# A convolution and gated two-layer product: the first product's rest term as a pair of 64-row matmuls

## The chip, the core and the metric

The kernel runs on one core of one Trainium2 chip. A core has five engines that run side by side and meet only at semaphores: TensorE (PE in the profile, with its weight loads listed apart as PEld), VectorE (DVE), ScalarE (ACT), GpSimd (POOL), and SyncE (SP), which here only issues DMAs. PE multiplies a stationary block of weights (up to 128 rows by 128 columns) with moving columns and adds into PSUM. The metric is the device time of one execution in microseconds (us), lower is better. Before the change it is 2808.53 us, the median of three runs from 2807.76 to 2809.02.

## What is computed

```python
w = softmax(weight)                      # 8 heads, 7 taps each
x = causal_convolution(x, w)             # 8 x 4096 tokens, 192 channels, 24 per head
x = x.reshape(32768, 192)
h = x @ w_in                             # 192 x 2048
P = a[0] + a[1] * h + a[2] * h**2 + a[3] * h**3
Q = 1.0 + abs(b[0]) * abs(h) + abs(b[1]) * h**2
out = (P / (Q + 1e-6)) @ w_out           # 2048 x 192
```

## The kernel before

The tokens go in 64 chunks of 512. For each chunk the convolution is done on PE as band matrices (`conv_part`, L259): nine blocks of up to 58 tokens by six groups of 32 channels. Each matmul fills 32 columns of the array only, at `tile_position=(0, 32 * j)`. Half 0 has four groups, side by side on four column tiles, and gives 128 channels; half 1 has two groups on two column tiles and gives the last 64. In the trace each of these float32 matmuls stands as two instructions, and so does each of the second product's.

PE takes the first product in float32r, a shorter form of float32. So both of its factors are kept as two parts, a leading one and the rest: `wh_t` and `wl_t` for w_in, and for the convolved chunk ACT writes the leading part (`conv_evac_act`, L267, tiles xh0 and xh1) and DVE the rest (`conv_evac_dve`, L273 and L277). For the first 128 channels the parts are `xh0` (called A) and `xl` (L). For the last 64 channels one tile, `xh1` (B), holds the leading part in rows 0 to 63 and the rest in rows 64 to 127. The host lays out w_in's last 64 rows twice, so `wh_t[:, i, 1]` and `wl_t[:, i, 1]` hold the same 64 rows in both halves, and one pass over 128 rows multiplies both parts of B by one part of the weights.

The 2048 columns of w_in are taken in eight units of 256, two halves of 128 each. `gemm1(k, j)` (L289) makes half j of unit k: five full passes of 128 rows by 512 columns into one half of the PSUM tile hp, of which there are two. After that ACT, POOL and DVE work out P / (Q + 1e-6) for the unit in twelve or so steps of 128 x 1024 elements (L328 to L379), and `gemm2` (L306) multiplies the result with w_out, 64 float32 matmuls of 192 columns a chunk, spread between the units of the first product.

The order on PE, ACT, DVE and POOL is written out by hand as a list of steps: START (the first two chunks, with the weights' conversion from float64 in steps `wi..` and `wo..`), PLAN (one round, a chunk long, repeated), END. `g10a.0 ... g10b.0` is the first product's two halves of unit 0, `c1a.0` a third of the convolution's half 1, `xh1.0` and `xl1.0` its two evacuations by ACT and DVE. The order on SP is not in these lists: it is what the framework's scheduler makes of it. SP carries the loads of x (`load_x`, L158 and L159, into two buffers xs in turn, each needed again a round after it is filled or later) and the stores of the result (L314). In a round, `xl1.0` stands four steps before `g10a.0`, the first step that reads B:

```python
... c1a.0 c1b.0 L4.1 c1c.0 p6.1 m3.1 g17a.1 A6.1 g17b.1
e3.1 u6.1 xh1.0 B6.1 g24d.1 g3.1 p7.1 g25a.1 Q6.1 g25b.1 v6.1 Y4.1 g25c.1 hs7.1 xl1.0 g25d.1 m4.1
g10a.0 B7.1 u7.1 A7.1 g10b.0 e4.1 L5.1 g26a.1 ...
```

Of the kernel before, what the change touches and what calls it, by code (L numbers as in the profile page):

```python
# [10 lines left out]
F32 = mybir.dt.float32  # L11
F32R = mybir.dt.float32r
# [4 lines left out]
ALU = mybir.AluOpType  # L17
# [7 lines left out]
P = 128  # L25
CH = 512
# [11 lines left out]
F64_MIN = float(np.uint32(0x38000000).view(np.float32))  # L38


# The order in which the engines take the steps of one chunk of tokens: step, unit or half,
# piece; after the point, how many chunks later than the first step of its chunk it is taken.
PLAN = """
c0a.0 L7.2 m6.2 u1.1 g12a.1 O1.2 A1.1 e6.2 g12b.1 B1.1 Q0.1 g6.2 g20a.1 hs2.1 c0b.0 v1.1 g20b.1 Y7.2
c0c.0 p2.1 L0.1 m7.2 g13a.1 B2.1 u2.1 g13b.1 e7.2 A2.1 g20c.1 g7.2 A3.1 g20d.1 Q1.1 g21a.1 v2.1 Y0.1
# [6 lines left out]
g11a.0 m5.1 p0.0 B0.0 g11b.0 e5.1 u0.0 L6.1 g27a.1 g5.1 hs1.0 g27b.1 g27c.1 p1.0 v0.0 Y6.1 g27d.1  # L52
"""

# How a unit's cubic begins. H: on VectorE, from PSUM; U: on GpSimd; V: on ScalarE, then GpSimd.
MODES = "UUUHVUUV"

# The first two rounds, with the preparation of the weights (wi: w_in, wo: w_out; step, piece);
# after the point the chunk.
START = """  # L60
wia0.0 c0a.0 wim0.0 wis0.0 c1a.0 wid0.0 wia1.0 c1b.0 wio0.0 wim1.0 wir0.0 c1c.0 wis1.0 c0b.0 c0c.0
xh1.0 wid1.0 wia2.0 wih0.0 xl1.0 wio1.0 xh0.0 wir1.0 wim2.0 wid2.0 wia3.0 wil0.0 wia4.0 xl0.0 wis2.0
# [13 lines left out]
L6.0 e5.0 u0.1 wor7.0 hs1.1 g5.0 p1.1 Y6.0 v0.1 wor4.0  # L76
"""

# What remains after the last full round; after the point the chunks from the end.
END = """  # L80
u1.2 L7.3 m6.3 B1.2 O1.3 c0a.1 g12a.2 A1.2 g12b.2 Q0.2 e6.3 hs2.2 c0b.1 g6.3 Y7.3 g20a.2 v1.2 A2.2
B2.2 c0c.1 g20b.2 m7.3 g20c.2 p2.2 g20d.2 g21a.2 e7.3 g13a.2 g13b.2 g21b.2 g7.3 g21c.2 u2.2 xh0.1
# [26 lines left out]
def kernel(  # L109
# [12 lines left out]
    nc = tc.nc  # L122
# [3 lines left out]
    xpool = ctx.enter_context(tc.tile_pool(name="xpool", bufs=2))  # L126
# [9 lines left out]

    nc.scalar.preload_act_table_set("natural_log_exp_and_others")

# [1 line left out]
    wb_t = const.tile([P, NG, BW], F32, name="wb_t")  # L140
    mb_t = const.tile([P, NG, BW], F32, name="mb_t")
    wr_t = const.tile([P, NG, KT], F32, name="wr_t")
# [15 lines left out]
        nc.sync.dma_start(out=t[0:BLK, 0:3 * XF // 4], in_=xa[c])  # L158
        nc.sync.dma_start(out=t[BLK:, 3 * XF // 4:], in_=xb[c])  # L159

# [1 line left out]
    mx = const.tile([P, NG], F32, name="mx")  # L162
    sm = const.tile([P, NG], F32, name="sm")
    nc.vector.tensor_reduce(out=mx, in_=wr_t, axis=AX.X, op=ALU.max)
# [7 lines left out]
    nc.vector.tensor_tensor(out=wb_t, in0=wb_t, in1=mb_t, op=ALU.mult)  # L172
    nc.vector.tensor_tensor(out=wb_t, in0=wb_t, in1=sm[:, :, None].broadcast_to([P, NG, BW]), op=ALU.mult)

# [1 line left out]
    cf = const.tile([P, 6], F32, name="cf")  # L176
    nc.vector.tensor_scalar(cf[:, 0:4], ab_t[:, 0:4], -1.0, None, ALU.mult)
    nc.scalar.activation(out=cf[:, 4:6], in_=ab_t[:, 4:6], func=AF.Abs)
# [15 lines left out]
        scales.append(reg)  # L194
    r_be0, r_sq1, r_a3 = scales

# [1 line left out]
    # In integers: the upper word's digits, rebiased, then the lower word's, rounded, added.  # L198
    wh_t = const.tile([P, UPC, 2, 2, P], F32R, name="wh_t")
    wl_t = const.tile([P, UPC, 2, 2, P], F32R, name="wl_t")  # L200
    wo_t = const.tile([P, FT, D], F32, name="wo_t")
# [16 lines left out]
    def prep(which, i, step):  # L218
        w = pieces[which, i]
        if step == "a":  # L220
            ad = apool.tile([P, 2, W // 2], I32, name="ad")
            w["a"], w["d"] = ad[:, 0, 0:w["n"]], ad[:, 1, 0:w["n"]]
            nc.scalar.activation(out=w["a"].bitcast(F32), in_=w["hi"].bitcast(F32), func=AF.Abs)
        elif step == "d":
            nc.scalar.activation(out=w["d"], in_=w["lo"], func=AF.Identity, scale=2.0 ** -29)
        elif step == "m":
            nc.vector.tensor_scalar(w["a"].bitcast(F32), w["a"].bitcast(F32), F64_MIN, None, ALU.max)  # L227
        elif step == "s":
            if which == "i":
                w["t"] = apool.tile([P, W // 2], F32, name="tr")  # L230
            else:
                w["t"] = wo_t[:, 2 * i:2 * i + 2].rearrange("p f m -> p (f m)")
            nc.vector.tensor_scalar(w["t"].bitcast(U32), w["a"].bitcast(U32), 3, 0x3FFFFFF8,  # L233
                                    ALU.logical_shift_left, ALU.bitwise_and)
        elif step == "o":
            t = w["t"].bitcast(U32)
            nc.vector.scalar_tensor_tensor(out=t, in0=w["hi"], scalar=0xC0000000, in1=t,  # L237
                                           op0=ALU.bitwise_and, op1=ALU.bitwise_or)
        elif step == "r":
            t = w["t"].bitcast(I32)  # L240
            nc.gpsimd.tensor_tensor(out=t, in0=t, in1=w["d"], op=ALU.add)
        elif step == "h":
            nc.scalar.copy(out=wh_t[:, i].rearrange("p a b c -> p (a b c)"), in_=w["t"])
        elif step == "l":
            nc.vector.tensor_tensor(out=wl_t[:, i].rearrange("p a b c -> p (a b c)"), in0=w["t"],  # L245
                                    in1=wh_t[:, i].rearrange("p a b c -> p (a b c)").bitcast(F32), op=ALU.subtract)

# [1 line left out]
    def stat(c, blk, g):  # L249
        t = xs_buf[c % 2].rearrange("p (m b g) -> p m b g", m=32, b=NBLK)  # L250
        return t[:, :, blk, g]
# [10 lines left out]
    X = {}  # L262

    def conv_evac_act(c, half, cps):
        xh = xpool.tile([P, CH], F32R, name=f"xh{half}")
        n = 32 * len(GROUPS[half])
        nc.scalar.copy(out=xh[0:n], in_=cps[0:n])  # L267
        X[c, "AB"[half]] = xh

    def conv_evac_dve(c, half, cps):  # L270
        if half == 0:
            xl = xpool.tile([P, CH], F32R, name="xl")
            nc.vector.tensor_tensor(out=xl, in0=cps, in1=X[c, "A"].bitcast(F32), op=ALU.subtract)  # L273
            X[c, "L"] = xl
        else:
            xh = X[c, "B"]
            nc.vector.tensor_tensor(out=xh[64:P], in0=cps[0:64], in1=xh[0:64].bitcast(F32), op=ALU.subtract)  # L277

# [1 line left out]
    H = {}  # L280

    def gemm1(k, j):
        c, i = divmod(k, UPC)
        xhA, xlA, xB = X[c, "A"], X[c, "L"], X[c, "B"]
        if j == 0:
            H[k] = ps_h.tile([P, 2, CH], F32, name="hp")
        terms = ((wh_t, 0, xhA), (wh_t, 0, xlA), (wh_t, 1, xB), (wl_t, 0, xhA), (wl_t, 1, xB))
        for n, (w, part, x) in enumerate(terms):
            nc.tensor.matmul(H[k][:, j, :], lhsT=w[:, i, part, j, :], rhs=x, start=(n == 0), stop=(n == len(terms) - 1))  # L289

# [1 line left out]
    G = {}  # L292
    O = {}

# [18 lines left out]
        nc.scalar.copy(out=ob, in_=O.pop((c, pair))[:, :, 0:D])  # L313
        nc.sync.dma_start(out=out_v[c, pair], in_=ob)  # L314

# [1 line left out]
    st = {}  # L317

    def flat(k):
# [59 lines left out]
        nc.vector.scalar_tensor_tensor(out=g, in0=st[k]["y"], scalar=2.0, in1=g, op0=ALU.subtract, op1=ALU.mult)  # L379
        del st[k], H[k]  # L380

# [1 line left out]
    unit_steps = {"hs": step_hs, "p": step_p, "u": step_u, "v": step_v, "A": step_A, "B": step_B, "Q": step_Q,  # L383
                  "L": step_L, "Y": step_Y, "m": step_m, "e": step_e, "g": step_g}
    CP = {}
# [9 lines left out]
    def take(kind, n, piece, c):  # L395
        if kind in ("g2", "O"):
            if c > NCH or c < 0:
                return
            if kind == "g2":
                if c > 0:  # L400
                    gemm2(c - 1, n, piece)
            elif c > 0:
                out_evac(c - 1, n)
        elif 0 <= c < NCH:
            if kind == "g1":
                gemm1(c * UPC + n, piece)
            elif kind == "c":
                conv_step(c, n, piece)
            elif kind == "xh":
                conv_evac_act(c, n, CP[c, n])  # L410
            elif kind == "xl":
                conv_evac_dve(c, n, CP.pop((c, n)))
            else:
                unit_steps[kind](c * UPC + n)

# [1 line left out]
    def steps(text):  # L417
        return [(kind, int(n), "abcd".find(piece) if piece else 0, int(c))
                for kind, n, piece, c in re.findall(r"(g1|g2|w[io][a-z]|[A-Za-z]+)(\d)([a-d]?)\.(\d+)", text)]

    order = steps(START)
# [3 lines left out]
    with tc.manual_schedule(engines={E.PE, E.Activation, E.DVE, E.Pool}):  # L425
        load_x(0)
        for i in range(UPC):
            load_w("i", i)
        load_x(1)
        for i in range(UPC):  # L430
            load_w("o", i)
        for kind, n, piece, c in order:
            if kind[0] == "w":
                prep(kind[1], n, kind[2])
            else:
                take(kind, n, piece, c)
# [52 lines left out]
```

## Time and profile before

| what | us |
|---|---|
| runs, median of three | 2808.53 |
| the profiled execution: span from its first to its last instruction (no other time of it is given) | 2807.8 |
| second product, busy (L306, 8128 instructions) | 1420.8 |
| first product, leading weights by A and B, busy (L289, 2048 passes) | 872.9 |
| first product, rest weights by A and B, busy (2048 passes) | 637.7 |
| first product, leading weights by the rest of A, busy (1024 passes) | 405.5 |
| convolution, busy (L259, 6876 instructions) | 195.3 |

The busy times of PE's groups overlap, since one matmul starts before the end of the one ahead of it; what one costs is read from how far apart the starts lie. A row of the timeline has the start and the duration in us, the engine, the line, the operation, the tiles (written <- read), and how many instructions in a row it covers; in square brackets stand the idle time of the engine before it and what ended that. A row of a window has its length and then, for each engine, the busy time and the number of instructions. A row of the waits has the total in us, how many, and the longest.

### The profile page before, as it was taken

What the parts mean: (1) busy time and instruction counts of PE and PEld (TensorE: products, weight loads), DVE (VectorE), ACT (ScalarE), POOL (GpSimd) and SP (SyncE); (2) the same over time, 40 slices, a digit from 0 to 9 for tenths busy, and PEclk for the clock granted to TensorE, in tenths of its full rate; (3) what the DMA queues carried; (4) which work ended last, traced back from release to release, by engine and by line L of the source; (5) the groups of instructions that cost most, each with busy time, mean ns of one, the idle gap of its engine ahead of it and who ended that gap; (6) DMA issues with size and microseconds to landing.
All of it is one profiled execution on the core that took longest, in us unless ns stands there. A gap on an engine that the chain in (4) does not pass through costs nothing.

```text
span 2807.8 us, 50193 instructions
## 1 busy us (share of the span) xinstructions
PE 2748.3 (98%) x20224; PEld 2458.2 (88%) x20224; DVE 2683.3 (96%) x2309; ACT 2688.4 (96%) x2990; POOL 2684.4 (96%) x1304
## 2 busy tenths in 40 slices
PE   4799999999999999999999999999999999999999
PEld 3688988988889889889889888888898898898888
DVE  8999999999999999999999999999999999999998
ACT  6899999999999999999999999999999999999997
POOL 6899999999999999999999999999999999999996
PEclk8899999999999999999999999999999999999999
DMA  4000000000000000000000000000000000000000
GB/s 136 10 16 25 22 16 25 22 16 25 21 17 22 19 22 22 19 22 22 16 25 22 16 25 22 16 22 19 22 22 19 22 22 16 25 22 16 25 9 15
DMA packets 49193, 64.43 MB, mean 23 GB/s; under 512 B 4672, under 2 KB 43840, under 8 KB 48960
## 3 DMA queue, kind: packets, MB, share of 16 engines
q1 hardware_dynamic: 48960, 61.22, 7.9%
q8 instruction: 159, 2.61, 0.4%
q14 instruction: 74, 0.61, 0.1%
HBM read 36.03 MB, written 25.17 MB: 22 GB/s over the span
## 4 chain that ended last, share of the span: by engine, by line
PE 96%; DVE 2%; issue 1%; ACT 0%; DMA 0%; SPq 0%; ACTq 0%; DVEq 0%
PE op L306 48%; PE hp L289 42%; PE cps L259 6%; DVE ad L227 0%; PE cps L306 0%; DVE t L351 0%; DVE wl_t L245 0%; DMA g<-in_w_in 0%; DVE g L370 0%; DVE y L375 0%; DVE tr L233 0%; DVE tr L237 0%; DVE wo_t L233 0%; DVE g L379 0%; DVE wo_t L237 0%
## 5 line engine op out<-in xcount | busy, mean ns | idle before, releaser
L306 PE MATMUL op<-wo_t,g 128*128 128x192 f32 x8128 | 1420.8, 326 | 0.0
L306 PEld LDWEIGHTS op<-wo_t,g 128*128 128x128 f32 x8128 | 1344.6, 189 | 43.9
L360 POOL TENSOR_TENSOR A<-A,B 128x1024 f32<-128x1024 f32 x512 | 1219.2, 2388 | 28.4 <-ACT B L357 26.1
L347 POOL TENSOR_TENSOR t<-t,hs 128x1024 f32<-128x1024 f32 x448 | 1077.9, 2406 | 48.6 <-ACT hs L334 16.3
L289 PE MATMUL hp<-xh,wh_t 128*128 128x512 f32 x2048 | 872.9, 426 | 45.9 <-DVE t L351 41.4
L370 DVE SCALAR_TENSOR_TENSOR g<-t,cf,y 128x1024 f32<-128x1024 f32 x512 | 654.4, 1278 | 57.0 <-ACT y L366 46.6
L351 DVE SCALAR_TENSOR_TENSOR t<-t,cf,hp 128x1024 f32<-128x1024 f32 x512 | 652.5, 1274 | 32.7 <-POOL t L347 29.9
L379 DVE SCALAR_TENSOR_TENSOR g<-y,g 128x1024 f32<-128x1024 f32 x512 | 626.9, 1224 | 17.5
L289 PE MATMUL hp<-xh,wl_t 128*128 128x512 f32 x2048 | 637.7, 393 | 0.0
L375 DVE SCALAR_TENSOR_TENSOR y<-A,y 128x1024 f32<-128x1024 f32 x512 | 625.5, 1222 | 0.0
L363 ACT ACTIVATE B<-A 128x1024 f32<-128x1024 f32 x512 | 547.0, 1069 | 0.2 <-POOL A L360 0.2
L366 ACT ACTIVATE y<-B 128x1024 f32<-128x1024 f32 x512 | 528.8, 1033 | 15.6 <-DVE g L379 14.6
L354 ACT ACTIVATE A<-hp 128x1024 f32<-128x1024 f32 x512 | 528.0, 1031 | 15.8 <-PE hp L289 15.7
L357 ACT ACTIVATE B<-hp 128x1024 f32<-128x1024 f32 x512 | 528.7, 1033 | 0.0
L289 PEld LDWEIGHTS hp<-xh,wh_t 128*128 128x128 f32 x2048 | 388.8, 190 | 124.4 <-DVE t L351 32.6
L334 ACT COPY hs<-hp 128x1024 f32<-128x1024 f32 x448 | 457.2, 1020 | 35.4 <-PE hp L289 34.1
L289 PEld LDWEIGHTS hp<-xh,wl_t 128*128 128x128 f32 x2048 | 388.2, 190 | 87.5
L289 PE MATMUL hp<-xl,wh_t 128*128 128x512 f32 x1024 | 405.5, 396 | 2.4 <-DVE xl L273 2.4
L340 POOL TENSOR_SCALAR t<-hs,cf 128x1024 f32<-128x1024 f32 x320 | 389.6, 1217 | 10.8 <-ACT hs L334 3.9
L328 ACT ACTIVATE t<-hp,cf 128x1024 f32<-128x1024 f32 x192 | 214.7, 1118 | 25.3 <-PE hp L289 22.8
L259 PEld LDWEIGHTS cps<-wb_t,xs 128*32 128x32 f32 x6876 | 162.5, 149 | 65.8 <-issue 64.3
L289 PEld LDWEIGHTS hp<-xl,wh_t 128*128 128x128 f32 x1024 | 195.4, 191 | 23.7 <-DVE xl L273 2.9
(49 smaller groups left out, 632.6 us busy)
## 6 DMA issues: line engine op xcount, KB each, us to landing
out<-ob SPq DMA_DIRECT2D x128, 192.0 KB, 2.0
xs<-in_xa SPq DMA_DIRECT2D x64, 324.0 KB, 3.9
xs<-in_xb SPq DMA_DIRECT2D x64, 108.0 KB, 3.7
g<-in_w_in SPq DMA_DIRECT2D x8, 512.0 KB, 9.4
g<-in_w_out SPq DMA_DIRECT2D x8, 384.0 KB, 9.3
wb_t<-in_wband SPq DMA_DIRECT2D x1, 174.0 KB, 2.4
mb_t<-in_mband SPq DMA_DIRECT2D x1, 174.0 KB, 2.4
wr_t<-in_wrep SPq DMA_DIRECT2D x1, 21.0 KB, 1.9
```

Of the source, the lines that this page charges most:

```text
L289: nc.tensor.matmul(H[k][:, j, :], lhsT=w[:, i, part, j, :], rhs=x, start=(n == 0), stop=(n == len(terms) - 1))
L306: nc.tensor.matmul(op[:, t, 0:D], lhsT=g[:, f % 2, tok:tok + P], rhs=wo_t[:, f, :], start=(f == 0 and t == 0), stop=(f == FT - 1 and t == 1))
L347: nc.gpsimd.tensor_tensor(out=t, in0=t, in1=st[k]["hs"], op=ALU.mult)
L351: nc.vector.scalar_tensor_tensor(out=t, in0=t, scalar=a1, in1=flat(k), op0=ALU.add, op1=ALU.mult)
L354: nc.scalar.activation(out=tile_of(k, "A", work), in_=flat(k), func=AF.Abs, scale=r_be0)
L357: nc.scalar.activation(out=tile_of(k, "B", work), in_=flat(k), func=AF.Square, scale=r_sq1)
L360: nc.gpsimd.tensor_tensor(out=st[k]["A"], in0=st[k]["A"], in1=st[k]["B"], op=ALU.add)
L363: nc.scalar.activation(out=st[k]["B"], in_=st[k]["A"], func=AF.Ln, bias=C_Q)
L366: nc.scalar.activation(out=tile_of(k, "y", ps_y), in_=st[k]["B"], func=AF.Exp, scale=-1.0)
L370: nc.vector.scalar_tensor_tensor(out=G[k].rearrange("p a b -> p (a b)"), in0=st[k]["t"], scalar=a0, in1=st[k]["y"], op0=ALU.add, op1=ALU.mult)
L375: nc.vector.scalar_tensor_tensor(out=y, in0=st[k]["A"], scalar=C_Q, in1=y, op0=ALU.add, op1=ALU.mult)
L379: nc.vector.scalar_tensor_tensor(out=g, in0=st[k]["y"], scalar=2.0, in1=g, op0=ALU.subtract, op1=ALU.mult)
```

## The change

The line of `wl_t` for the last 64 channels gets a new upper half: after a unit's `wl_t` has been made, a DMA copies rows 0 to 63 of `wh_t[:, i, 1]` over it. B gets a new lower half: the leading part is copied by a DMA to rows 64 to 127. One full pass of `wl_t[:, i, 1]` with B now gives leading weights by leading x (upper half) plus rest weights by leading x (lower half), for which there were two passes. The rest of the last 64 channels goes to a tile of its own, `xm`: DVE writes rows 0 to 63, a DMA copies them to rows 64 to 127. A unit's last term, leading weights by xm, is a pair of 64-row matmuls after the second half's passes: rows 0 to 63 of the array for half 0, rows 64 to 127 for half 1, each of 512 columns into its own half of hp. The product of the rest weights with xm, which the pass before took along, is left out. So a unit has eight full passes and a pair instead of ten full passes. The lists START, PLAN and END stay.

```diff
         elif step == "l":
             nc.vector.tensor_tensor(out=wl_t[:, i].rearrange("p a b c -> p (a b c)"), in0=w["t"],
                                     in1=wh_t[:, i].rearrange("p a b c -> p (a b c)").bitcast(F32), op=ALU.subtract)
+            nc.sync.dma_start(out=wl_t[0:64, i, 1].bitcast(F32), in_=wh_t[0:64, i, 1].bitcast(F32))
...
         nc.scalar.copy(out=xh[0:n], in_=cps[0:n])
+        if half == 1:
+            nc.sync.dma_start(out=xh[64:P].bitcast(F32), in_=xh[0:64].bitcast(F32))
         X[c, "AB"[half]] = xh
...
-            xh = X[c, "B"]
-            nc.vector.tensor_tensor(out=xh[64:P], in0=cps[0:64], in1=xh[0:64].bitcast(F32), op=ALU.subtract)
+            xm = xpool.tile([P, CH], F32R, name="xm")
+            nc.vector.tensor_tensor(out=xm[0:64], in0=cps[0:64], in1=X[c, "B"][0:64].bitcast(F32), op=ALU.subtract)
+            nc.sync.dma_start(out=xm[64:P].bitcast(F32), in_=xm[0:64].bitcast(F32))
+            X[c, "M"] = xm
...
-        terms = ((wh_t, 0, xhA), (wh_t, 0, xlA), (wh_t, 1, xB), (wl_t, 0, xhA), (wl_t, 1, xB))
+        terms = ((wh_t, 0, xhA), (wh_t, 0, xlA), (wl_t, 0, xhA), (wl_t, 1, xB))
         for n, (w, part, x) in enumerate(terms):
-            nc.tensor.matmul(H[k][:, j, :], lhsT=w[:, i, part, j, :], rhs=x, start=(n == 0), stop=(n == len(terms) - 1))
+            nc.tensor.matmul(H[k][:, j, :], lhsT=w[:, i, part, j, :], rhs=x, start=(n == 0), stop=False)
+        if j == 1:
+            xlB = X[c, "M"]
+            for half in range(2):
+                rows = slice(64 * half, 64 * half + 64)
+                nc.tensor.matmul(H[k][:, half, :], lhsT=wh_t[rows, i, 1, half, :], rhs=xlB[rows], start=False, stop=True,
+                                 tile_position=(64 * half, 0))
```

On PE, this is the place in a round where a new chunk's unit 0 begins, before the change. The rows are PE's matmuls in program order, with the line, the tiles and the shape; xh_1572 is xh0 (A) of the new chunk and xh_1689 its xh1 (B); the number behind a tile only tells buffers apart, and 128x512 is the output's shape. First stand the last two passes of unit 7 of the chunk before.

```order
L289 MATMUL hp<-xh_1205,wl_t 128x512
L289 MATMUL hp<-xh_1322,wl_t 128x512
L306 MATMUL op<-wo_t,g 128x192 x10
L289 MATMUL hp<-xh_1572,wh_t 128x512
L289 MATMUL hp<-xl,wh_t 128x512
L289 MATMUL hp<-xh_1689,wh_t 128x512
L289 MATMUL hp<-xh_1572,wl_t 128x512
L289 MATMUL hp<-xh_1689,wl_t 128x512
```

The same place of the changed kernel; A of the new chunk is xh_1592 here and B xh_1709. What a row waits for is shown where it waits: DMAHW6 and DMAHW0 are the semaphores of DMAs, here those of the copies into B and into xm.

```order
L294 MATMUL hp<-xh_1339,wl_t 128x512
L299 MATMUL hp<-xm,wh_t 128x512 x2
L317 MATMUL op<-wo_t,g 128x192 x10
L294 MATMUL hp<-xh_1592,wh_t 128x512 [waits DVE_49,PE_49]
L294 MATMUL hp<-xl,wh_t 128x512
L294 MATMUL hp<-xh_1592,wl_t 128x512
L294 MATMUL hp<-xh_1709,wl_t 128x512 [waits DMAHW6_49,Activation_49]
L294 MATMUL hp<-xh_1592,wh_t 128x512
L294 MATMUL hp<-xl,wh_t 128x512
L294 MATMUL hp<-xh_1592,wl_t 128x512
L299 MATMUL hp<-xm,wh_t 128x512 [waits DVE_49]
L299 MATMUL hp<-xm,wh_t 128x512 [waits DMAHW0_49]
```

The pass of leading weights by B is gone from each half; the pair stands behind the second half's passes and ahead of the second product's matmuls, and the second one of it waits for the DMA into xm. The other engines keep their rows in their order.

On SP, these are the DMAs of one round before the change, in the order in which SP issues them: loads of x, then two stores.

```order
L158 DMA xs_97<-in_xa 64x1296
L159 DMA xs_97<-in_xb 64x432
L314 DMA out<-ob 128x2x192 x2
```

And of the changed kernel, with the copies into B (L270) and into xm (L281):

```order
L158 DMA xs_97<-in_xa 64x1296
L270 DMA xh_969<-xh_969 64x512
L159 DMA xs_97<-in_xb 64x432
L281 DMA xm<-xm 64x512
L325 DMA out<-ob 128x2x192 x2
```

The copy into B stands between the two loads of x, so the second load waits behind it; the copy into xm stands after both, ahead of the stores.

## The prediction

> **What bounds the kernel now.** I read the page's busy shares first, then one round of the loop (one chunk of 512 tokens) in the view of busy time by window, then the chain that ended last.
>
> ```profile
> span 2807.8 us, 50193 instructions
> PE 2748.3 (98%) x20224; PEld 2458.2 (88%) x20224; DVE 2683.3 (96%) x2309; ACT 2688.4 (96%) x2990; POOL 2684.4 (96%) x1304
> core 0: us, PE busy (x) PEld busy (x) DVE busy (x) ACT busy (x) POOL busy (x), PEclk, DMA share, GB/s
> 1480.00:1522.67 42.67, 42.67 (x318) 38.25 (x316) 41.05 (x36) 41.62 (x47) 41.52 (x21) 1.00 0.08 21
> 57.00:100.00 43.00, 19.12 (x73) 13.46 (x71) 42.80 (x41) 29.02 (x38) 34.55 (x20) 0.65 0.00 0
> PE 96%; DVE 2%; issue 1%; ACT 0%; DMA 0%; SPq 0%; ACTq 0%; DVEq 0%
> 114.73 3.90 PE op L306 x24
> 2675.40 3.90 PE op L306 x24
> ```
>
> Four engines stand at 96 to 98% of the span, so the shares alone don't say which one sets the time. The round does: PE is busy 42.67 of 42.67 us at granted clock 1.00, while ACT, POOL and DVE have 1.05, 1.15 and 1.62 us free. The chain agrees (96% PE), and its two rows, the same group of 24 matmuls, lie 2560.67 us apart: 60 rounds of 42.68 us. In the window from 57 to 100 us, in which the weights are still being prepared, PE has work for 19.12 of 43.00 us only; about 12 of the 512 units fall where PE waits like that. I count 500 units in which each ns on PE is a ns of the end.
>
> ```profile
> ACT hs L334 <- PE hp L289: 34.1, 67, 2.9
> ACT t L328 <- PE hp L289: 22.8, 62, 2.6
> ACT A L354 <- PE hp L289: 15.7, 61, 0.3
> PEld cps L259 <- issue: 64.3, 252, 7.2
> ```
>
> The waits say the same from the other side: ACT's three waits for the first product sum to 72.6 us, 1.13 us a chunk, which is nearly all that it has free. The fourth row matters most for this change: 252 times, four a chunk, PE's weight loads stood still for nothing that the profile names, 0.26 us each in the mean. All stand before the convolution (L259), the only place that uses a part of the array.
>
> **What PE loses and gains, per unit.** Ten full passes of 512 columns become eight, and two matmuls on 64 rows each are added, one for each half of the unit. The price of a full pass comes from the cadence of starts, since the durations overlap (mean 393 to 426 ns each):
>
> ```profile
> 1508.69 1.46 PE L306 MATMUL op<-wo_t,g 128*128 128x192 f32 x8
> 1510.08 0.59 PE L259 MATMUL cps<-wb_t,xs 128*32 128x58 f32 x24
> 1510.61 0.50 PE L289 MATMUL hp<-xh,wh_t 128*128 128x512 f32 x1
> 1510.95 0.39 PE L289 MATMUL hp<-xl,wh_t 128*128 128x512 f32 x1
> 1511.87 0.39 PE L289 MATMUL hp<-xh,wh_t 128*128 128x512 f32 x1
> 1491.29 2.11 PE L306 MATMUL op<-wo_t,g 128*128 128x192 f32 x12
> 1493.33 1.29 PE L259 MATMUL cps<-wb_t,xs 128*32 128x58 f32 x36
> 1494.88 0.40 PE L289 MATMUL hp<-xl,wh_t 128*128 128x512 f32 x1
> ```
>
> From 1510.95 to 1511.87 four passes start: 0.23 us a pass. So two passes give back **0.46 us** a unit. If the pair cost nothing that would be 3.68 us a chunk.
>
> The pair isn't in this trace, but a neighbour is: the convolution also runs on parts of the array (four or two column tiles of 32 instead of two row tiles of 64). Its price is read between the full-width matmuls on both sides. A matmul of the second product takes 3.90/24 = 0.1625 us. The eight from 1508.69 leave room for the next start at 1509.99; the second pass of the first product starts at 1510.95, so the first one streamed from 1510.72. The convolution between took 0.73 us, for 24 matmuls on four tiles, 6 waves. In the same way the twelve from 1491.29 end at 1493.24, the next first pass streams from 1494.65: 1.41 us for 36 matmuls on two tiles, 18 waves. Twelve more waves cost 0.68 us, 0.057 us each; take six of them from 0.73 us and a **fixed 0.39 us** is left for each visit to the tiled array. Full width to full width has no such price:
>
> ```profile
> 1486.41 2.76 PE L306 MATMUL op<-wo_t,g 128*128 128x192 f32 x16
> 1489.23 0.40 PE L289 MATMUL hp<-xl,wh_t 128*128 128x512 f32 x1
> 1510.08 0.46 PEld L259 LDWEIGHTS cps<-wb_t,xs 128*32 128x32 f32 x24 [0.23 <-issue]
> 1510.61 0.19 PEld L289 LDWEIGHTS hp<-xh,wh_t 128*128 128x128 f32 x1
> 1510.71 0.19 PEld L289 LDWEIGHTS hp<-xl,wh_t 128*128 128x128 f32 x1
> ```
>
> Sixteen from 1486.41 end at 1489.01, and 1489.23 less one pass is 1489.00. What the 0.39 us is made of can be seen in the load rows: on the way in the load stands still for 0.23 us instead of being done under the running matmul; on the way out no load lies under the last small matmuls either, and the two first full-width loads follow each other at 0.10 us, uncovered. So the array empties before its shape changes, and the first load of each shape lies open.
>
> The Trainium skill, "TensorEngine Tiling (Array Packing)", Key Properties, has the rule that changing the tiling mode, not only the tile, drains TensorE. These rows agree for column tiles (0.39 us a visit); no row here shows it for row tiles, and by the rule the pair would pay as the convolution does.
>
> The pair streams 512 columns once if its two matmuls run side by side, 0.23 us. They go to different rows of the array and different halves of hp, and the convolution's four tiles (6 waves for 24 matmuls) show that tiles do run side by side. Cost of the pair: 0.39 + 0.23 = 0.62 us from the fit; up to 0.10 us more, since the loads on the way in are of 128 columns here and of 32 there. Ends for the unknown: 0.23 us (no fixed price, side by side) and 0.95 us (fixed price with the longer load, one after the other, 0.72 + 0.23). I take **0.64 us**, just above the nearest row's 0.62. Against 0.46 us removed that is **+0.18 us a unit**, 1.44 us a chunk: the round goes to 44.1 us, still PE's, with the other engines waiting longer. 500 x 0.18 = 90 us.
>
> **The copies.** Two copies of 128 KB a chunk go on SP's queue, and PE, DVE and ACT keep their order. The copy of xh1 may start at 1495.88, behind the load of xa and ahead of that of xb; the xs buffer that these fill is wanted a round later, so their delay costs nothing. The copy of xm is the near one:
>
> ```profile
> 1495.30 0.58 ACT L267 CAST xh<-cps 64x512 fp32r<-64x512 f32 x1
> 1499.25 0.69 DVE L277 TENSOR_TENSOR xh<-cps,xh 64x512 fp32r<-64x512 f32 x1
> 1500.06 0.53 PE L289 MATMUL hp<-xh,wh_t 128*128 128x512 f32 x1
> out<-ob SPq DMA_DIRECT2D x128, 192.0 KB, 2.0
> xs<-in_xb SPq DMA_DIRECT2D x64, 108.0 KB, 3.7
> PE hp L289 <- DVE t L351: 41.4, 9, 7.7
> ```
>
> DVE ends xm at 1499.94. By the landing time of the out rows (2.0 us) it lands at 1501.94, by that of xb (3.7 us) at 1503.64. PE begins unit 0 of the new chunk at 1500.06, 0.18 us later after the dearer unit 7, runs eight passes (1.84 us) and wants the pair at 1502.08. So the wait is 0 to 1.6 us a chunk, with the second product's matmuls queued behind it. I take 0: the copy is small, as the out rows are, and a slower PE lets DVE and POOL, which have less free than they would then get, reach xm earlier. Nor is a gain possible there. The eight copies into wl_t delay the first units by at most one landing each; PE waits 41.4 us there for DVE anyway, in 9 waits, so I take +1 us. **Sum:** 2807.8 + 90 + 1 = 2898.8 us of span; the median of the runs shown, 2808.53, is 0.7 us above this profile's span, the only time that it has. Forecast **2899 us**, own range 2868 (0.12 us a unit) to 2933 (0.25 us).
>
> **Rivals.** *No fixed price for row tiles.* The pair's weights are loaded under the last full pass, and the pair costs 0.23 us: PE falls to 42.67 - 8 x 0.23 = 40.83 us a chunk. Then ACT (41.62 busy), POOL and DVE bound it, with handoffs: 41.8 to 42.4, say 42.1 us, which is 0.57 us x 61 = 35 us less: **2773 us** (2755 to 2792). For it: rows of the array are not columns, and no row here shows a row tile; the two kinds of full-width matmul change over freely. Against it: the load for 32 columns had as much reason to go ahead and stood still 252 times. It decides on the other side as soon as the pair costs under 0.46 us.
>
> The Trainium skill, "TensorE: Matmul & The Clock Gate", Part 3, The mechanism, lets a weight load run ahead of matmuls in flight if it goes to another row group or to the spare weight buffer. That speaks for this rival; the 0.23 us in the load rows speaks against it for column tiles, and no run here shows it for row tiles.
>
> *One side only.* The array empties going in, but the second product's weights are loaded ahead on the way out: half of 0.39, so the pair costs 0.43 to 0.48 us, from -0.03 to +0.02 us a unit: 2793 to 2818 us, about **2800**. The uncovered loads after both convolution visits speak against it.
>
> *Dearer.* The pair runs one after the other (0.18 + 0.23 = 0.41 us a unit, **3005 us**), or xm lands as late as xb (1.6 x 61 = 95 us on top, **2995**), or a part of either: 2935 to 3010. Four column tiles in one wave and the out rows' 2.0 us speak against both.
>
> **How the numbers follow.** Forecast 0.58, no fixed price 0.22, one side 0.07, dearer 0.13. The range from 2768 to 2940 holds the forecast, the one side, the upper half of the second case and the foot of the last: about 0.8. Under 0.2% (5.6 us) can't be told from no change. Faster: 0.22 + 0.03 = 0.25; within: 0.03; slower: 0.58 + 0.13 + 0.01 = 0.72.
>
> **What would show it.** In the changed profile a middle round should be about 44.1 us with PE still at 100%, and ACT's waits for hp longer by about 1.4 us a chunk. Before the pair the load row should stand still about 0.2 us for "issue", some 500 times more than 252; the pair's two matmuls should start within some ns of each other, and the next second-product matmul some 0.64 us after the eighth pass would have given way. If the pair's loads lie under the last full pass, the rival without a fixed price holds, and the round is 41.8 to 42.4 us with PE below 98%. If the second of the pair starts 0.23 us after the first, they don't run side by side. A wait of PE for a DMA at each chunk's first pair would show the copy late.

## The result, and the profile after

The changed kernel takes **2914.19 us** (median of four runs, 2913.65 to 2915.19) against 2808.62 us (four runs) for the one before: 1.0377 times as long, with a 95% interval of 1.0363 to 1.0392. The profiled execution's span grew by 104.1 us. The first fence is from its page, its view of busy time by window, its waits, and two rows of ACT's timeline, one round apart.

```profile
span 2911.9 us, 50587 instructions
PE 2842.2 (98%) x20224; PEld 2323.4 (80%) x20224; DVE 2678.6 (92%) x2309; ACT 2695.8 (93%) x2990; POOL 2685.0 (92%) x1304
1480.00:1524.10 44.10, 44.10 (x318) 36.11 (x317) 41.02 (x36) 41.73 (x47) 41.51 (x20) 1.00 0.10 27
PEld hp L299 <- issue: 185.4, 512, 0.7
PEld op L317 <- issue: 120.0, 496, 0.2
PEld cps L260 <- issue: 64.1, 253, 7.1
PEld hp L294 <- DMA xh<-xh: 17.3, 1, 17.3
PE hp L294 <- DMA wl_t<-wh_t: 16.6, 1, 16.6
PEld hp L299 <- DMA xm<-xm: 2.1, 4, 1.0
2262.58 0.56 ACT L268 CAST xh<-cps 64x512 fp32r<-64x512 f32 x1
2306.68 0.57 ACT L268 CAST xh<-cps 64x512 fp32r<-64x512 f32 x1
```

A round takes 44.10 us, and PE is busy in all of it. Where PE never stops, its busy share can't tell how long a round is; the length is read from ACT's cast of the last 64 channels, which comes once a round (the last two rows; the median over all rounds is 44.11 us, before the change 42.67). The other engines' busy times are those of before within 0.3%, so their shares fell from 96% to 92 or 93% only because the span is longer. The loads now stand still for "issue" in two new places, on the way into each pair (512 times, 0.36 us) and on the way out of it (496 times, 0.24 us); the convolution's row is as it was. Two single waits of 17 us for the same stall, at the very start, are new too.

One pair in PE's timeline, with the weight loads of another pair under it:

```profile
1511.52 0.61 PE L294 MATMUL hp<-xh,wl_t 128*128 128x512 f32 x2
1512.07 0.50 PE L299 MATMUL hp<-xm,wh_t 64*128 64x512 f32 x2
1512.50 3.52 PE L317 MATMUL op<-wo_t,g 128*128 128x192 f32 x20
1516.09 0.39 PE L294 MATMUL hp<-xl,wh_t 128*128 128x512 f32 x1
1501.16 0.19 PEld L299 LDWEIGHTS hp<-xm,wh_t 64*128 64x128 f32 x2 [0.36 <-issue]
1501.59 0.79 PEld L317 LDWEIGHTS op<-wo_t,g 128*128 128x128 f32 x5 [0.24 <-issue]
```

Two full passes from 1511.52 at 0.23 us each would give way at 1511.98. The second product's twenty matmuls (0.1625 us each) and the next unit's first pass (0.23 us) end at 1516.09, so they streamed from 1512.61. The pair cost 0.63 us. Its two matmuls together last 0.50 us where a single pass lasts 0.39 us or more with its modelled end, so they run side by side; in the trace the second starts 3 ns after the first.

How the 104 us grew can be followed at ACT's logarithm, one a unit. Its first and its last row before the change, then after it:

```profile
33.96 1.07 ACT L363 ACTIVATE B<-A 128x1024 f32<-128x1024 f32 x1
2792.80 1.05 ACT L363 ACTIVATE B<-A 128x1024 f32<-128x1024 f32 x1
```

```profile
46.03 1.08 ACT L374 ACTIVATE B<-A 128x1024 f32<-128x1024 f32 x1
2896.71 1.05 ACT L374 ACTIVATE B<-A 128x1024 f32<-128x1024 f32 x1
```

Unit 0 is already 12.1 us late, and the other 511 add 91.8 us, 0.18 us each. So there are two main losses, one at the start and one in each unit. A third is small: in five rounds the copy of xm came late, and these took 44.40 to 45.28 us, 3.2 us more in all.

### The profile page after: what moved, and what is told of

Same layout as the page of the kernel before. It is cut to its first block, busy times and chain, and to the rows that moved or that the text cites. A ratio compares the mean times of both kernels' runs of the same rounds, so it can differ in the third digit from the quotient of the medians.

```text
span 2911.9 us, 50587 instructions
## 1 busy us (share of the span) xinstructions
PE 2842.2 (98%) x20224; PEld 2323.4 (80%) x20224; DVE 2678.6 (92%) x2309; ACT 2695.8 (93%) x2990; POOL 2685.0 (92%) x1304
## 4 chain that ended last, share of the span: by engine, by line
PE 96%; DVE 2%; DMA 1%; issue 1%; ACT 0%; SPq 0%; ACTq 0%; DVEq 0%
PE op L317 49%; PE hp L294 33%; PE hp L299 7%; PE cps L260 6%; DMA xm<-xm 0%; PE cps L317 0%; DMA g<-in_w_out 0%; DVE wl_t L245 0%; DVE t L362 0%; DMA g<-in_w_in 0%; DMA wl_t<-wh_t 0%; DVE ad L227 0%; DVE g L381 0%; DVE y L386 0%; DVE wo_t L233 0%
## 5 line engine op out<-in xcount | busy, mean ns | idle before, releaser
L317 PE MATMUL op<-wo_t,g 128*128 128x192 f32 x8128 | 1473.8, 333 | 0.0
L317 PEld LDWEIGHTS op<-wo_t,g 128*128 128x128 f32 x8128 | 1305.9, 190 | 124.9 <-issue 120.0
L294 PE MATMUL hp<-xh,wl_t 128*128 128x512 f32 x2048 | 646.3, 397 | 16.6 <-DMA wl_t<-wh_t 16.6
L294 PE MATMUL hp<-xh,wh_t 128*128 128x512 f32 x1024 | 468.6, 458 | 39.8 <-DVE t L362 36.4
L299 PE MATMUL hp<-xm,wh_t 64*128 64x512 f32 x1024 | 259.0, 498 | 0.9 <-DMA xm<-xm 0.7
L294 PEld LDWEIGHTS hp<-xh,wh_t 128*128 128x128 f32 x1024 | 194.7, 190 | 77.1 <-DVE t L362 28.3
L299 PEld LDWEIGHTS hp<-xm,wh_t 64*128 64x128 f32 x1024 | 96.8, 184 | 187.6 <-issue 185.4
```

Source lines behind the costliest of these rows:

```text
L299: nc.tensor.matmul(H[k][:, half, :], lhsT=wh_t[rows, i, 1, half, :], rhs=xlB[rows], start=False, stop=True, tile_position=(64 * half, 0))
L317: nc.tensor.matmul(op[:, t, 0:D], lhsT=g[:, f % 2, tok:tok + P], rhs=wo_t[:, f, :], start=(f == 0 and t == 0), stop=(f == FT - 1 and t == 1))
```

## The experiments

### e1: the same pair at full width

```diff
-                rows = slice(64 * half, 64 * half + 64)
-                nc.tensor.matmul(H[k][:, half, :], lhsT=wh_t[rows, i, 1, half, :], rhs=xlB[rows], ...
-                                 tile_position=(64 * half, 0))
+                nc.tensor.matmul(H[k][:, half, :], lhsT=wh_t[:, i, 1, half, :], rhs=xlB, ...
```

> The two 64-row matmuls become two full passes over 128 rows (wh_t's two equal halves by xm's two equal halves, so this last term is counted twice); every copy, wait and order stays. Theory (the price is the change of the array's shape, 0.40 us a visit, and the start lost 12 us to copies): a unit has ten full passes as before the change, the round returns to 42.7 us, about 2914 - 500 x 0.18 = 2824 us, and the start stays 12 us late. Rival (the copies, their DMA traffic or their waits make each round dearer): stays at 2905 to 2914 us.

Measured: 2835.86 us (2835.17 to 2838.45), 1.01 times the kernel before (1.0085 to 1.0116), 78 us less than the changed kernel with the same copies and the same operands. That answers the rival: the array's shape makes the loss. It is 12 us above the expected 2824, though. Its window, two of its waits, and the copy of xm with unit 0's pair in that window:

```profile
1480.00:1522.88 42.88, 42.88 (x318) 38.14 (x317) 40.93 (x36) 41.57 (x47) 41.52 (x21) 1.00 0.10 27
PEld hp L298 <- DVE y L384: 21.9, 56, 0.6
PEld hp L294 <- DMA xh<-xh: 16.7, 1, 16.7
1519.06 0.46 SPq L281 DMA_DIRECT2D xm<-xm  x1
1521.44 0.70 PE L298 MATMUL hp<-xm,wh_t 128*128 128x512 f32 x2
```

The round is 42.9 us, not 42.67: once a chunk (56 rows) the pair's load stands still, up to 0.6 us. The wait is put down to a DVE step that ends at about the same time, but the pair reads nothing of that step. What it waits for is the copy of xm, issued at 1519.06 and landing 2.2 us later in this run's median; unit 0's pair began at 1521.44. With PE faster, the copy is late after all.

### e2: one full pass in place of the pair

```diff
-            for half in range(2):
+            for half in range(1, 2):
...
+                nc.tensor.matmul(H[k][:, half, :], lhsT=wh_t[:, i, 1, half, :], rhs=xlB, ...
```

> The pair becomes one full pass into half 1 only (half 0 is left without its rest term, half 1 gets it twice): the price that a pair without any change of shape would have, 0.23 us a unit. Theory (only the visit is dear): PE needs 40.85 us a chunk, less than ACT's 41.7, so the round is set by ACT, POOL and DVE at 41.8 to 42.4 us and the time is 2773 + 12 = 2785 us (2765 to 2805). Rival (PE's order and waits hold the round whatever the pair costs): a round of 42.6 us or more, 2815 us or more.

Measured: 2773.59 us (2772.22 to 2775.93), 0.9874 of the kernel before (0.9859 to 0.9889), although the start is late here as well.

```profile
1480.00:1521.92 41.92, 41.24 (x309) 36.61 (x308) 40.83 (x36) 41.46 (x47) 41.41 (x21) 1.00 0.10 28
PEld hp L298 <- DVE y L384: 53.9, 50, 1.8
POOL 63%; issue 16%; DVE 9%; PE 7%; ACT 4%; DMA 1%; SPq 0%; POOLq 0%; ACTq 0%; DVEq 0%
```

PE is no longer busy all the time (41.24 of 41.92 us), and ACT and POOL are within 0.5 us of the round. The whole 0.68 us stands in one place, before unit 0's pass with xm, which waits for the copy as in e1. The chain that ended last (the third row) runs mainly through POOL (63%), no longer through PE (7%). This is what the idea of the change is worth where the last term costs one stream: 0.73 us a chunk.

### e3: both matmuls on the same rows

```diff
-                rows = slice(64 * half, 64 * half + 64)
+                rows = slice(0, 64)
...
-                                 tile_position=(64 * half, 0))
+                                 tile_position=(0, 0))
```

> Both 64-row matmuls go to rows 0 to 63 of the array, one after the other. Theory (the pair ran side by side, its two starts 3 ns apart): one more stream of 0.23 us a unit, 2914 + 505 x 0.23 = 3030 us. Rival (the two already stream one after the other, and the 0.62 us holds two streams and a smaller fixed price): no change, 2914 us.

Measured in one run: 3028.53 us. In its timeline the two last longer together:

```profile
1503.33 0.73 PE L299 MATMUL hp<-xm,wh_t 64*128 64x512 f32 x2
```

0.73 against 0.50 us: one more stream. So the pair on two row tiles did run side by side, and all of its 0.63 us but one stream of 0.23 us is the fixed price, 0.40 us.

### e8: two visits a unit

```diff
-        if j == 1:
+        if True:
...
-            for half in range(2):
+            for half in (j,):
```

> Each of the two 64-row matmuls follows its own half's passes, so that a unit has two visits to the row tiles with one matmul each instead of one visit with two. Theory (0.40 us fixed a visit and 0.23 us a stream): one more visit and one more stream, 0.63 us a unit, 2914 + 505 x 0.63 = 3232 us. Rival (the price lies in the two matmuls and their loads, not in the visit; e3 has given one stream at 0.23 us): no more than one stream, 3030 us.

Measured in one run: 3231.08 us. Two casts one round apart lie at 49.11 us, the median is 49.13:

```profile
2263.41 0.57 ACT L268 CAST xh<-cps 64x512 fp32r<-64x512 f32 x1
2312.52 0.57 ACT L268 CAST xh<-cps 64x512 fp32r<-64x512 f32 x1
PEld hp L299 <- issue: 378.1, 1024, 0.7
```

Twice as many standstills, of the same length (0.37 us), and 5.02 us a chunk more, 0.63 us a unit. With e3's stream of 0.23 us taken off, one more visit costs 0.40 us, though there is one matmul in it instead of two.

### e4 and e5: the loads of w_out behind the copies

In the changed kernel SP issues these DMAs in this order (its part of the timeline; the second column is the time from the first to the last issue of a row, the count stands at the end). Behind them stand one of SP's waits and two of PE's rows:

```profile
11.97 11.43 SPq L214 DMA_DIRECT2D g<-in_w_out  x8
23.46 0.50 SPq L270 DMA_DIRECT2D xh<-xh  x1
24.31 0.49 SPq L281 DMA_DIRECT2D xm<-xm  x1
25.37 1.52 SPq L247 DMA_DIRECT2D wl_t<-wh_t  x2
SPq L214 <- DMA g<-in_w_in: 7.3, 6, 1.7
16.66 0.63 PE L294 MATMUL hp<-xh,wl_t 128*128 128x512 f32 x1
33.90 0.77 PE L294 MATMUL hp<-xh,wl_t 128*128 128x512 f32 x1 [16.61 <-DMA wl_t<-wh_t]
```

The eight loads of w_out hold the queue until 23.4 us. Most of that is no wait for buffers: six times, 7.3 us in all, SP waits for one of w_in's loads to land, and in the trace each DMA here waits on the semaphore of the one eight before it. Steps that free a buffer end 0.7 us of SP's waits. The copies stand behind the loads: the first one's data were ready at 11.87 (ACT's cast), it is issued at 23.46, and then it takes 9.8 us to land, against 3.5 us in the median. PE waits in the middle of its first unit for 16.6 us. e4 puts five of the eight loads behind copies, e5 all of them; this is e5's edit.

```diff
-        for i in range(UPC):
-            load_w("o", i)
+        later = {1: (2, 0), 2: (1, 6), 3: (3, 4), 4: (7, 5)}
...
+                if kind == "wil" and n in later:
+                    for i in later[n]:
+                        load_w("o", i)
```

> Five of the eight loads of w_out are issued behind the copies into wl_t, one each, instead of all eight ahead of the first copy. Theory (the 12 us at the start come from the copies standing behind these loads on SP's queue): PE's first unit ends some 12 us earlier, 2914 - 10 to 12 = 2903 us. Rival (it is the copies' own landing times, 2 to 3.5 us each, or the start is held by the weights' conversion anyway): no more than 3 us gained, 2911 us or more.

> All eight loads of w_out are issued behind the first copies of x, xm and wl_t; only w_in's loads stay ahead of them. e4 moved five loads and its first unit came 5 of the 12 us earlier (41.08 against 46.03 us for the first logarithm on ACT, 33.96 before the change). Theory (the copies queue behind the loads' data, whichever stand ahead): another 3 to 5 us, first logarithm at 36 to 38 us, total 2903 to 2907 us. Rival (what is left of the delay is the copies' own landing times): first logarithm stays near 41 us, total 2910 us.

Measured: e4 2910.62 us (2908.46 to 2912.02), 4 us gained, fewer than the 10 to 12 expected. Its first logarithm stands at 41.08 us, 7 us later than before the change, with three loads still ahead of the copies. e5 gives 2904.85 us (2903.74 to 2906.22), 9 us less than the changed kernel, and its first logarithm is back within 0.8 us of the kernel before:

```profile
34.77 1.08 ACT L374 ACTIVATE B<-A 128x1024 f32<-128x1024 f32 x1
```

So the order of SP's queue makes the late start: with the same copies ahead of the loads of w_out, 11 of the 12 us at this logarithm are gone, although PE still waits 5.8 us for a copy in its first unit. Of the 12 us the total got 9 back.

### e6, e7, e9, e10, e11: fewer visits by the convolution

If a visit costs 0.39 us, the kernel before pays it four times a chunk too. Half 0 of the convolution is done in thirds, c0a, c0b and c0c; these kernels put all three in one visit in PLAN and leave START and END. e7 does it in the kernel before, e6 in the changed one:

```diff
-c0a.0 L7.2 m6.2 u1.1 g12a.1 ... g20a.1 hs2.1 c0b.0 v1.1 g20b.1 Y7.2
-c0c.0 p2.1 L0.1 m7.2 g13a.1 ...
+c0a.0 c0b.0 c0c.0 L7.2 m6.2 u1.1 g12a.1 ... g20a.1 hs2.1 v1.1 g20b.1 Y7.2
+p2.1 L0.1 m7.2 g13a.1 ...
```

> The kernel before the change, with the same merging of the convolution's visits and nothing else. Theory: PE needs 42.67 - 0.78 = 41.9 us a chunk, just above ACT's 41.6, so the round is 41.9 to 42.3 us: 25 to 47 us less than 2808, 2761 to 2783 us, faster than both kernels. Rival (the merged visit holds up the matmuls that ACT and DVE wait for next, so that it is lost again): 2800 us or more.

> The changed kernel, with the three thirds of the convolution's half 0 taken in one visit instead of three in each round of PLAN. Theory (each visit to a tiled array has a fixed price of 0.39 us on PE, and PE sets the round): two visits less a chunk, 2 x 0.39 x 61 = 48 us, 2914 - 48 = 2866 us, round 43.3 us. Rival (the 0.39 us is covered or comes back as another wait, since the pair's visits stay): no change, 2910 us or more.

Measured: e7 2831.93 us (2831.1 to 2832.34), 1.0085 times the kernel before; e6 2908.64 us (2907.19 to 2910.63), 5.5 us less than the changed kernel where 48 were expected. e7's rival won, and e6 is close to its own. In e7 the visits did go, and more came back, as three of its waits and two rows of ACT's and DVE's timelines show:

```profile
PEld hp L289 <- DVE t L351: 94.4, 68, 9.0
PE hp L289 <- DVE t L351: 84.9, 71, 8.6
PEld cps L259 <- issue: 36.9, 128, 7.0
1524.70 1.01 ACT L334 COPY hs<-hp 128x1024 f32<-128x1024 f32 x1 [1.10 <-PE hp L289]
1526.68 1.28 DVE L370 SCALAR_TENSOR_TENSOR g<-t,cf,y 128x1024 f32<-128x1024 f32 x1 [1.19 <-ACT y L366]
```

The standstills fell from 252 to 128, but the two thirds now run ahead of unit 2's passes. ACT waits 1.10 us for unit 2, DVE 1.19 us behind ACT, and PE a few us later, before unit 4, for the hp that these steps release. The rounds take 43.1 us in the median, although ACT and DVE had 1.05 and 1.62 us free a chunk.

e9 puts the merged visit where c0c stood, so that unit 2 comes earlier rather than later; e10 keeps e7's place and moves two pieces of the second product ahead of unit 3; e11 is e9's order in the changed kernel.

```diff
-c0a.0 L7.2 m6.2 ... hs2.1 c0b.0 v1.1 g20b.1 Y7.2
-c0c.0 p2.1 L0.1 ...
+L7.2 m6.2 ... hs2.1 v1.1 g20b.1 Y7.2
+c0a.0 c0b.0 c0c.0 p2.1 L0.1 ...
```

> The kernel before the change with the three thirds of half 0 in one visit, now at the place of the last third instead of the first. e7 saved the two visits (its waits of PE's loads for nothing fell from 252 to 128) and lost 1.3 us a chunk in a new wait of unit 3 for hp, because the two thirds that stood ahead of it had moved away. Theory (fixed price per visit; only the place was wrong): unit 3 begins no earlier than before, PE needs 41.9 us a chunk, 25 to 45 us less than 2808: 2763 to 2783 us. Rival (hp's release holds any round that is shorter on PE, here unit 2's): 2800 us or more.

> The kernel before the change with the merged visit at the place of the first third, and two pieces of the second product (16 matmul instructions, 1.3 us... of which 8 a piece) moved ahead of unit 3 in place of the two thirds that went. Theory: unit 3's wait for hp (0.75 to 1.3 us a chunk in e7) is filled, 2763 to 2783 us. Rival as for e9: the wait only moves to another unit, 2800 us or more.

> The changed kernel with the merged visit at the place of the last third, as e9 has it for the kernel before. Theory (0.39 us a visit, PE sets the round, and e6 lost its gain only by delaying unit 2): two visits less a chunk and no new wait, 2 x 0.39 x 61 = 48 us less, 2866 us, round 43.3 us. Rival (with the pair's visits in the round the merging brings little, as e6 had it): 2900 us or more.

Measured: e9 **2775.7 us** (2773.9 to 2776.53), 0.9881 of the kernel before (0.9865 to 0.9898); e10 2834.14 us; e11 2871.54 us (2870.93 to 2872.09), 43 us less than the changed kernel. Two casts one round apart in e9, and the place of its merged visit on PE:

```profile
423.96 0.58 ACT L267 CAST xh<-cps 64x512 fp32r<-64x512 f32 x1
466.09 0.57 ACT L267 CAST xh<-cps 64x512 fp32r<-64x512 f32 x1
1494.05 1.46 PE L306 MATMUL op<-wo_t,g 128*128 128x192 f32 x8
1495.44 1.33 PE L259 MATMUL cps<-wb_t,xs 128*32 128x58 f32 x72
1497.03 0.40 PE L289 MATMUL hp<-xl,wh_t 128*128 128x512 f32 x1
```

The same two casts in e11:

```profile
446.12 0.57 ACT L268 CAST xh<-cps 64x512 fp32r<-64x512 f32 x1
489.55 0.57 ACT L268 CAST xh<-cps 64x512 fp32r<-64x512 f32 x1
```

In the median a round takes 42.12 us in e9 and 43.42 us in e11, 0.55 and 0.69 us less than without the merging: 0.28 and 0.35 us for each of the two visits, less than the 0.39 expected. The merged visit itself did save nearly that. Read as in the prediction, the eight matmuls from 1494.05 end at 1495.35 and the next first pass streams from 1496.80: 1.45 us against three times 0.73, 0.37 us for each visit saved. The rest of it came back elsewhere in e9's round, and where wasn't traced. e10 failed because my reading of e7 had named the wrong unit: the wait is unit 4's, not unit 3's. Unit 2 holds the hp that unit 4 gets, and in e10 unit 3 moved by the matmuls put ahead of it while unit 4 came no earlier.

## Why the prediction was right, point by point

**The bound.** As predicted PE set every round, before and after. e2 shows how near the next bound lies: with PE at 41.24 us of work the round stops at 41.92, with POOL on the chain, and the range forecast for "no fixed price" (41.8 to 42.4) held.

**The price of the pair.** Read from the convolution as 0.64 us, measured as 0.63; the excess of 0.18 us a unit is what the rounds (1.44 us longer, eight units) show. The fixed 0.39 us turned out as 0.40 us (the pair with e3) and 0.40 (e8); for the convolution's visits e9 and e11 gave back 0.28 and 0.35 of it. That row tiles would cost what column tiles do was an analogy, and it held. The standstill on the way in was forecast at about 0.2 us and is 0.36; the one of 0.24 us on the way out was not among the signs forecast. The rule of the Trainium skill, "TensorEngine Tiling (Array Packing)", Key Properties, that a change of the tiling mode drains TensorE, agrees for row tiles too: the pair's load stood still 0.36 us, 512 times.

**The rivals.** "No fixed price for row tiles" fell with e1, and none of the 512 pairs had its load run ahead. "One side only" fell with the two new rows of waits, 0.36 us going in and 0.24 us coming out. Of "dearer", the pair one after the other was excluded by e3, and the late copy came only now and then in the changed kernel (five rounds, 3.2 us in all). The price put on the first of these doesn't follow from its own terms: 0.41 us for 500 units is 205 us on 2808, 3013 us and not 3005.

**The copies in the rounds.** Taking 0 was right but for these 3.2 us, and for the reason given: at a PE pace of 44.10 us DVE reaches xm earlier. It ends xm 1.0 us before unit 0's first pass (1514.71 and 1515.72), where before the change it was 0.12 us. e1 shows the other side of it, 0.2 us a chunk at 42.9 us. It needed a slower PE to be true.

**The start.** This is the term that was mis-sized: "+1 us" for the copies at the start against 12.1 us measured. The step looked at the copies' landing time and at PE's waits for DVE, and not at what stands ahead of them on SP's queue. The waits for DVE took up little of it: they were to hide the delay and only fell from 41.4 to 36.4 us, beside 16.6 us of waiting for the copy. With 12.1 the sum would have been 2910 us of span against the measured 2911.9; the forecast was 2899.

**What stays open.** Why the 0.36 us on the way in and the 0.24 us on the way out differ wasn't tried, nor whether row tiles of another height cost the same. That the array empties at a change of shape is read from the loads that stand still; no run shows the emptying itself. What took back part of e9's gain is open too.

## What to carry to other kernels

A few matmuls on part of the array between full-width ones cost a visit, here 0.40 us, besides their stream. Two matmuls side by side on two tiles, in place of two full passes, pay only where such a visit saves more than 0.40 us of streaming; here it saved 0.23 us. So count the visits, and put what needs the same shape together, at a place where no other engine is waiting for what comes next: the same merging lost 23 us at one place in the order and gained 33 us at another.

A copy inside a kernel that goes on the queue of the loads stands behind all loads issued before it, also those that are themselves still waiting to be issued.

## What was not expected of the hardware

The price of a visit was about the same for two row tiles with one load each (0.40 us) and, by the prediction's fit, for two or four column tiles with 18 or 6 waves (0.39 us; 0.37 us in e9's merged visit), although the loads are of 128 columns in the one and 32 in the other.
